# Group 0 of a fused transformer block in half-width units, its first weights in pieces, and a new order on one Trainium2 core

## The chip, the cores and the metric

The kernel runs on one core of one Trainium2 chip. The metric is the device time of one execution in microseconds (us); the number given for the kernel before is the median of three runs. Five engines work side by side, each through its own list of instructions in order: PE (matmuls; its weight loads are listed as PEld), DVE (vector), ACT (scalar activations and copies), POOL, and SP, which here only issues DMAs. Semaphores tie the engines together.

## The reference

x is [1, 2048, 512] in bf16. The vector c gives six modulation vectors of 512 (shift, scale and gate for each of two halves).

```
mod = (silu(c) @ w_mod)            # sa, ca, ga, sb, cb, gb
h = layernorm(x) * (1 + ca) + sa
x = x + ga * attention(h)          # 32 heads of 16, window of 8 positions at distance 2
h = layernorm(x) * (1 + cb) + sb
x = x + gb * ((gelu(h @ w_gate) * (h @ w_up)) @ w_down)     # F = 1792

# attention: q, k, v = h @ wqkv; position s looks at s, s-2, ..., s-14 (masked below 0)
logits = sum over d of q[s] * k[s - 2w] / 4;  attn = softmax over the 8 w
o = sum over w of attn * v[s - 2w];  result o @ wo
```

## The kernel before, in words

The 2048 positions go in four groups of 512 (number sg), each of four chunks of 128. The 512 channels of q, k and v are taken in four quarters j (every fourth channel, `j::4`), so that each quarter holds four channels of all 32 heads on 128 partitions. For each group:

- LN1: DVE and ACT take the statistics of a chunk (DVE BN_STATS2, L395, or ACT's sum and sum of squares, L378 and L384), POOL makes rstd, DVE writes xn (L435). PE transposes (or a DMA does), and DVE or ACT write hT with modulation (L487; for group 0, in two halves of 256 positions, L503 and L505).
- q, k, v: op `qp.sg.blk.j` (blk 0, 1, 2 for q, k, v) is four matmuls of 128x512 into one PSUM bank (L554); ACT evicts it (`qkv.sg.blk.j`; q L568, k L570, v L572). In group 0 quarters 0 and 1 of q are done by halves, 16 matmuls of 128x256 (L536, ops `qph`).
- logits: `pq.sg.j` on DVE multiplies q with eight shifted views of k (L617, 128x4096, 2.28 us each); `lp` on PE sums over channels and quarters with matmuls on a quarter of the array each (L631, 8 for each j, "quad" matmuls below). The last of a group's four is called `lp.sg`.
- softmax: DVE mask L643, max L648, subtract L654, ACT exp L659, DVE sum L664 (`s1.sg`), reciprocal L670 (`ri.sg`), product L675 (`p.sg`). SP writes the result to DRAM (`est`, L687) and reads it back spread out (`PT`, L694). v goes the same way (`vst` L591, `V4` L599).
- `pv.sg.j` on DVE (L706), `o.sg.j` on PE (L720, quad), oT on ACT (L731), `x1p.sg.c` on PE with wo (L741), x1 on DVE (L750), then LN2.
- FFN, 14 tiles n of 128 of F: `g.sg.n` and `u.sg.n` on PE (L771, four matmuls of 128x512 each), gelu on ACT (`gl`, L803) and a copy (`ub`, L810), their product on DVE (`hh.sg.n`, L821), and after all 14 the product with w_down (`y`, L783, L794), with the output on DVE (L828, L835) and its DMA.

The gates ga and gb are multiplied into wo and w_down: `woS` (L361), and `WdS0` to `WdS6` (L356), seven instructions of 128x1024, two for each of the tiles Wd0 to Wd2 and one for Wd3. Wd0, Wd1 and Wd2 have no buffers of their own: they take those of wqkv's three blocks (pool wA), so that each of their DMAs (L243) waits until PE has used that block for the last time.

Limits: four PSUM banks for matmul results (`mm`), two for transposes and others (`att`), one for logits; three buffers each for `gl` and `ub`; four for the products `pq` and `pv` (`prod`).

All of this is written as some 120 generators ("threads") of operations. `ORDER` (L18) is a list of thread numbers: the issuer takes the next operation of the thread that stands next in the list and emits it. So ORDER alone sets in what sequence each engine, and each DMA queue, gets its instructions; an operation's time and place otherwise follow from semaphores.

In the first microseconds the DMAs bring x for group 0 in two halves, the first two blocks of w_mod (0 the shift, 1 the scale), wqkv's q block, x of group 1, then k's and v's blocks. PE turns w_mod's blocks into modT and 1 + scale (matmuls of one column, L286; ACT writes scl L294 and modT L291).

## Time and profile before

| | us |
| --- | --- |
| three runs | 238.48, 236.38, 237.23 |
| median | 237.23 |
| span of the profiled execution, first to last instruction | 234.1 |
| its whole time | not on the page; the median is 3.1 above its span |
| PE / DVE / ACT busy in the span | 228.9 / 167.5 / 148.4 |
| first qkv matmul, last PE instruction's end (about) | 8.88, 231.3 |
| first gate matmul of the FFN (g.0.0) | 65.23 |
| granted TensorE clock | 0.999 |

How to read what follows: a row of the order of time gives start, length, engine, line, operation, output <- inputs, shape and type, and the count of merged instructions; in square brackets stands the idle time before it and what ended that. The pipelined matmuls overlap in the records, so the time of several is taken from start to start. In the table of stretches the columns are the stretch and its length, then busy time (and instructions) of PE, PEld, DVE, ACT and POOL, the granted clock, the DMA engines' share and GB/s.

### The profile page before, as it was taken

What the parts mean: (1) busy time and instruction counts of PE and PEld (TensorE: products, weight loads), DVE (VectorE), ACT (ScalarE), POOL (GpSimd) and SP (SyncE); (2) the same over time, 40 slices, a digit from 0 to 9 for tenths busy, and PEclk for the clock granted to TensorE, in tenths of its full rate; (3) what the DMA queues carried; (4) which work ended last, traced back from release to release, by engine and by line L of the source; (5) the groups of instructions that cost most, each with busy time, mean ns of one, the idle gap of its engine ahead of it and who ended that gap; (6) DMA issues with size and microseconds to landing.
All of it is one profiled execution on the core that took longest, in us unless ns stands there. A gap on an engine that the chain in (4) does not pass through costs nothing.

```text
span 234.1 us, 3657 instructions
## 1 busy us (share of the span) xinstructions
PE 228.9 (98%) x1382; PEld 107.2 (46%) x1382; DVE 167.5 (72%) x240; ACT 148.4 (63%) x282; POOL 24.7 (11%) x37
## 2 busy tenths in 40 slices
PE   7899999999999999999999999999999999999995
PEld 2755454444544444444444444444444444444443
DVE  4889999999998999989999989916642122123222
ACT  4999996968995749928556961563568721466400
POOL 3210230892100000100000010000100000000000
PEclk9999999999999999999999999999999999999999
DMA  6998869999368280054404634100071001000011
GB/s 214 385 332 295 244 224 221 301 329 408 159 188 235 97 276 3 1 115 134 114 0 128 243 91 97 40 0 22 0 71 45 0 22 42 6 0 1 21 48 45
DMA packets 30313, 30.42 MB, mean 130 GB/s; under 512 B 14936, under 2 KB 26200, under 8 KB 30296
## 3 DMA queue, kind: packets, MB, share of 16 engines
q1 hardware_dynamic: 29760, 29.67, 41.3%
q10 hardware_dynamic: 536, 0.53, 0.6%
q8 instruction: 11, 0.18, 0.3%
q14 instruction: 6, 0.05, 0.1%
HBM read 22.78 MB, written 5.31 MB: 120 GB/s over the span
## 4 chain that ended last, share of the span: by engine, by line
PE 84%; DVE 9%; DMA 3%; ACT 1%; SPq 1%; issue 0%
PE g_ps L771 21%; PE u_ps L771 21%; PE y_ps L783 19%; PE qkv_ps L554 9%; PE x_ps L741 6%; DVE pq L617 5%; PE o_ps L720 3%; DMA x<-in_A_x_dram 3%; PE LTp L631 2%; PE y_ps L794 1%; DVE xn L435 1%; DVE st L395 1%; ACT qT L568 1%; DVE mx L648 1%; DVE LTp L654 1%; DVE e L675 1%
## 5 line engine op out<-in xcount | busy, mean ns | idle before, releaser
L771 PE MATMUL g_ps<-h,Wg 128*128 128x512 bf16 x224 | 57.5, 379 | 0.0
L771 PE MATMUL u_ps<-h,Wu 128*128 128x512 bf16 x224 | 57.5, 379 | 0.0
L803 ACT ACTIVATE gl<-g_ps 128x512 bf16<-128x512 f32 x56 | 33.8, 605 | 24.3 <-PE g_ps L771 23.4
L783 PE MATMUL y_ps<-Wd,hht 128*128 128x512 bf16 x210 | 47.0, 379 | 0.0
L821 DVE TENSOR_TENSOR hht<-gl,ub 128x512 bf16<-128x512 bf16 x56 | 23.2, 420 | 31.8 <-ACT ub L810 31.6
L810 ACT CAST ub<-u_ps 128x512 bf16<-128x512 f32 x56 | 33.0, 592 | 17.1 <-PE u_ps L771 17.1
L554 PE MATMUL qkv_ps<-hT,wqkv 128*128 128x512 bf16 x184 | 42.0, 380 | 0.2 <-ACT gR L349 0.2
L617 DVE TENSOR_TENSOR pq<-qT,kT 128x4096 bf16<-128x4096 bf16 x16 | 36.3, 2284 | 0.3 <-ACT kT L570 0.3
L706 DVE TENSOR_TENSOR pv<-PT,V 128x4096 bf16<-128x4096 bf16 x16 | 36.0, 2285 | 0.2 <-PE LTp L631 0.2
L771 PEld LDWEIGHTS <-Wg 128*128 128x128 bf16 x224 | 21.7, 98 | 27.2 <-issue 1.7
L771 PEld LDWEIGHTS <-Wu 128*128 128x128 bf16 x224 | 21.8, 98 | 26.8 <-issue 0.8
L783 PEld LDWEIGHTS <-hht 128*128 128x128 bf16 x210 | 20.4, 98 | 25.2 <-issue 0.8
L554 PEld LDWEIGHTS <-wqkv 128*128 128x128 bf16 x184 | 20.2, 114 | 18.8 <-issue 2.4
L426 POOL TENSOR_TENSOR rstd<-rstd,neghalf 128x4 f32<-128x4 f32 (+1 forms) x9 | 8.7, 971 | 122.3 <-DVE rstd L415 68.7
L828 DVE TENSOR_TENSOR ot<-y_ps,x 128x512 bf16<-128x512 f32 x15 | 10.2, 686 | 15.9 <-PE y_ps L783 15.9
L750 DVE TENSOR_TENSOR x<-x_ps,x 128x512 bf16<-128x512 f32 x16 | 10.8, 684 | 7.1 <-PE x_ps L741 7.1
L741 PE MATMUL x_ps<-woP,oT 128*128 128x512 bf16 x64 | 15.3, 379 | 0.0
L395 DVE BATCH_NORM_STATS2 st<-x 128x6 f32<-128x512 bf16 x19 | 12.5, 678 | 2.5 <-DMA x<-in_A_x_dram 2.5
L487 ACT ACTIVATE h<-h,modT,scl 128x512 bf16<-128x512 bf16 x12 | 9.0, 808 | 8.1 <-DMA h<-xn 8.1
L587 POOL COPY vh<-vT 128x64 bf16<-128x64 bf16 x3 | 12.0, 3992 | 16.7 <-ACT vT L572 16.7
L731 ACT CAST oT<-o_ps 128x512 bf16<-128x512 f32 x16 | 9.2, 600 | 6.6 <-PE o_ps L720 6.6
L378 ACT ACTIVATE gl<-x 128x512 bf16<-128x512 bf16 x13 | 8.3, 650 | 6.8 <-DVE x L750 6.0
(77 smaller groups left out, 186.8 us busy)
## 6 DMA issues: line engine op xcount, KB each, us to landing
V<-vscr SPq DMA_DIRECT2D x16, 526.0 KB, 6.7
wm<-in_w_mod_dram SPq DMA_DIRECT2D x5, 512.0 KB, 8.5
vscr<-vT SPq DMA_DIRECT2D x4, 528.0 KB, 7.4
out_dram<-ot SPq DMA_DIRECT2D x15, 128.0 KB, 1.7
Wg<-in_B_w_gate_dram SPq DMA_DIRECT2D x4, 448.0 KB
Wu<-in_B_w_up_dram SPq DMA_DIRECT2D x4, 448.0 KB, 7.6
wqkv<-in_A_wqkv_dram SPq DMA_DIRECT2D x3, 512.0 KB, 7.1
x<-in_A_x_dram SPq DMA_DIRECT2D x3, 512.0 KB, 8.0
```

Of the source, the lines that this page charges most:

```text
L395: nc.vector.bn_stats(out=k["st", c4][:], in_=src()[:, c4, :])
L554: nc.tensor.matmul(ps[:], lhsT=wqkv[blk][:, dt, j::4], rhs=B["hT", sg][:, :, dt, :], start=(dt == 0), stop=(dt == DT - 1))
L587: yield Op("POOL", 0.2, lambda: nc.gpsimd.tensor_copy(out=vh[:], in_=B["vT", sg][:, :, SG:VR]), after=[f"qkv.{sg}.2.3"], fire=f"vh.{sg}")
L617: nc.vector.tensor_tensor(out=pq[:], in0=_ap(B["qT", sg][:, j, :], [[0, W], [1, SG]]), in1=_ap(kT[:, j, sg * SG + 2:sg * SG + 2 + SG], [[2 ...
L706: nc.vector.tensor_tensor(out=t[:], in0=_ap(B["PT", sg][:, 0, :], [[SG, 2], [0, 4], [1, SG]]), in1=_ap(v[:, j, 0, :], [[8, 2], [VR, 4], [1 ...
L741: nc.tensor.matmul(ps[:], lhsT=B["oT", sg][:, j, c4 * P:(c4 + 1) * P], rhs=woP[:, j, :], start=(j == 0), stop=(j == 3))
L750: nc.vector.tensor_tensor(out=x[:, c4, :], in0=B["x1ps", sg, c4][:], in1=x[:, c4, :], op=ALU.add)
L771: nc.tensor.matmul(ps[:], lhsT=Wt[:, dt, ft * P:(ft + 1) * P], rhs=B["h2T", sg][:, :, dt, :], start=(dt == 0), stop=(dt == DT - 1))
L783: nc.tensor.matmul(ps[:], lhsT=B["hh", sg, ft][:, c4 * P:(c4 + 1) * P], rhs=B["Wd", ft // 4][:, ft % 4, :], start=(ft == 0), stop=(ft == F ...
L803: nc.scalar.activation(out=gl[:], in_=B["g", sg, ft][:], func=ACT.Gelu_apprx_tanh)
L810: nc.scalar.copy(out=ub[:], in_=B["u", sg, ft][:])
L821: nc.vector.tensor_tensor(out=hh[:], in0=B["gl", sg, ft][:], in1=B["ub", sg, ft][:], op=ALU.mult)
```

## The change

- **Loads.** x of group 0 comes as chunk 0, chunk 1 and chunks 2 and 3. Blocks 0 and 1 of w_mod become one tile `wm01` in two pieces, 768 KB and 256 KB, on SP's queue (before: one block on ACT's queue and one on SP's). wqkv's q block comes in four pieces of 128 KB, with x of group 1 between the first and the other three.
- **Modulation.** One PSUM bank takes all eight columns of shift and scale; ACT writes the scale, DVE the shift. The exp table is loaded earlier.
- **Group 0's transposes** go chunk by chunk, both halves into `att` banks.
- **Group 0's q, k, v** go in 12 units (half h of 256 positions, block blk, pair of quarters u): 8 matmuls of 128x256 into one bank, which ACT evicts at once as 128x2x256 (`qu.h.blk.u`, `qe.h.blk.u`; four of the units are issued in single steps, `quf`). pq.0.0 is split into two halves; pq.0.1 needs the units u = 0 of both halves, pq.0.2 and pq.0.3 those with u = 1.
- **ORDER** is a new list for the whole program.

The diff, cut to its core:

```diff
-            yield Op("SP", 0.47, ldx(0, 0, 2), fire="x0.0", lat=1.0)
+            yield Op("SP", 0.47, ldx(0, 0, 1), fire="x0.0", lat=1.0)
+            yield Op("SP", 0.47, ldx(0, 1, 2), fire="x0.1", lat=1.0)
+            yield Op("SP", 0.47, ldwm01(0, 3), take=[SL["prod"]], fire="wmA", lat=1.9)
+            yield Op("SP", 0.47, ldwm01(3, 4), fire="wmB", lat=0.6)
...
+            for dt in DT0:
+                yield Op("SP", 0.47, ld(wqkv[0][:, dt, :], wq_v[:, dt, 0:D]), fire=f"wqkv0.{dt}", lat=0.35)
...
+        yield Op("PE", 0.82, cols(0, 3), after=["wmA", "scT"], take=[SL["mm"]], fire="mpA")
+        yield Op("PE", 0.28, cols(3, 4), after=["wmB"], give=[SL["prod"]], fire="mpB")
+        yield Op("ACT", 0.12, lambda: nc.scalar.add(out=scl[:, 0:4], in_=B["mp"][:, 4:8], add=1.0), after=["mpB"], fire="mod1")
+        yield Op("DVE", 0.12, lambda: nc.vector.tensor_copy(out=modT[:, 0:4], in_=B["mp"][:, 0:4]), after=["mpB"], give=[SL["mm"]], fire="mod0")
...
+    DT0 = (0, 2, 1, 3)
+    DT1 = (1, 2, 0, 3)
+    def unit_mm(h, blk, u, dt, start, stop):
+        if start:
+            B["qu", h, blk, u] = T("mm", [P, 2, 256], F32, "qkv_ps")
+        for jj in range(2):
+            nc.tensor.matmul(B["qu", h, blk, u][:, jj, :], lhsT=wqkv[blk][:, dt, 2 * u + jj::4],
+                             rhs=B["hT", 0][:, 2 * h:2 * h + 2, dt, :], start=start and jj == 0, stop=stop and jj == 1)
+    def unit(h, blk, u):
+        def f():
+            for n, dt in enumerate(DT0):
+                unit_mm(h, blk, u, dt, n == 0, n == 3)
...
+    def fine(h, blk, us, dts):
+        for n, dt in enumerate(dts):
...
+    def unit_ev(h, blk, u):
+        def g():
+            ps = B["qu", h, blk, u]
+            o, w = 2 * u, slice(h * 256, h * 256 + 256)
+            if blk == 0:
...
+                nc.scalar.copy(out=B["qT", 0][:, o:o + 2, w], in_=ps[:])
+            elif blk == 1:
+                nc.scalar.copy(out=kT[:, o:o + 2, 16 + h * 256:16 + h * 256 + 256], in_=ps[:])
+            else:
+                nc.scalar.copy(out=B["vT", 0][:, o:o + 2, VH + h * 256:VH + h * 256 + 256], in_=ps[:])
...
+        mm = [chain(fine(0, 0, (0, 1), DT0), unit(0, 1, 0), unit(0, 1, 1)), chain(*[unit(*a) for a in v0]),
+              chain(fine(1, 0, (0,), DT1), *[unit(*a) for a in q1[1:]], *[unit(*a) for a in v1])]
...
+    def qkd(sg, blk, j):
+        return [f"qe.{h}.{blk}.{j // 2}" for h in range(2)] if sg == 0 else [f"qkv.{sg}.{blk}.{j}"]
...
+            parts = ((0, 256), (256, 512)) if sg == 0 and j in SPLIT else ((0, SG),)
...
+                dep = [q for blk in range(2) for q in qkd(sg, blk, j)[:1 if c1 < SG else 2]]
-    1, 26, 2, 10, 0, 10, 2, 1, 2, 0, 2, 10, 10, 2, 10, 0, 10, 9, 10, 2, 9, 20, 9, 10, 20, 10, 18, 20, 10, 21,
...
+    29, 2, 1, 2, 3, 0, 17, 39, 29, 29, 29, 0, 0, 18, 39, 29, 29, 29, 29, 39, 29, 39, 39, 2, 2, 29, 29, 29, 29, 39,
```

What the new list moves is seen in the engines' own orders. First ACT in the evictions of group 0 (gl<-x are the sums and squares for later groups' LN1, hT the evictions of group 1's transposes). Before:

```order
L378 ACTIVATE gl,sums<-x 128x512 x2
L572 CAST vT<-qkv_ps 128x512 x3
L487 ACTIVATE hT<-hTp,modT,scl 128x4x128 x4
L572 CAST vT<-qkv_ps 128x512
L570 CAST kT<-qkv_ps 128x512
L349 CAST gR<-gR_ps 128x128
```

and changed:

```order
L586 CAST kT<-qkv_ps 128x2x256
L508 ACTIVATE hT<-hTp,modT,scl 128x4x128 x2
L588 CAST vT<-qkv_ps 128x2x256 x2
L508 ACTIVATE hT<-hTp,modT,scl 128x4x128 x2
L588 CAST vT<-qkv_ps 128x2x256 x2
L399 ACTIVATE gl,sums<-x 128x512
L586 CAST kT<-qkv_ps 128x2x256
L405 ACTIVATE gl,sums<-x,sums 128x512
```

In both, a k eviction comes last of group 0. Before it holds quarter 3 for all 512 positions; now it holds quarters 2 and 3 for the first half (unit qu.0.1.1, on PE too the last of group 0), behind one sum (L399) of a later chunk.

Then DVE around the softmax of group 1 (Wd<-Wd,gB are the scalings WdS, two for a tile; hht the FFN's products). Before:

```order
L664 TENSOR_REDUCE ssum<-LTp 128x128
L670 RECIPROCAL rinv<-ssum 128x128
L675 TENSOR_TENSOR e<-LTp,rinv 128x2x4x128
L617 TENSOR_TENSOR pq<-qT,kT 128x4096 x2
L821 TENSOR_TENSOR hht<-gl,ub 128x512 x3
L706 TENSOR_TENSOR pv<-PT,V_884 128x4096 x2
L821 TENSOR_TENSOR hht<-gl,ub 128x512 x2
L706 TENSOR_TENSOR pv<-PT,V_884 128x4096 x2
L356 TENSOR_TENSOR Wd_1099<-Wd_1099,gB 128x1024
```

and changed:

```order
L733 TENSOR_REDUCE ssum<-LTp 128x128
L377 TENSOR_TENSOR Wd_1129<-Wd_1129,gB 128x1024
L739 RECIPROCAL rinv<-ssum 128x128
L377 TENSOR_TENSOR Wd_1129<-Wd_1129,gB 128x1024
L744 TENSOR_TENSOR e<-LTp,rinv 128x2x4x128
L683 TENSOR_TENSOR pq<-qT,kT 128x4096 x2
L890 TENSOR_TENSOR hht<-gl,ub 128x512 x2
L377 TENSOR_TENSOR Wd_1131<-Wd_1131,gB 128x1024 x2
L890 TENSOR_TENSOR hht<-gl,ub 128x512
L775 TENSOR_TENSOR pv<-PT,V_1013 128x4096 x2
```

The first two scalings move from behind all four pv of group 1 to behind its ssum, ahead of ri.1, p.1 and the logits products of group 2, and the next two to ahead of pv.1.0.

Last SP's queue at the same place (escr<-e is est.1, PT its way back, gB the gate's load). Before:

```order
L687 DMA escr_117<-e 128x1024
L243 DMA Wd_1099<-in_B_w_down_dram 128x4x512
L298 DMA gscr_115<-gR 4x128
L694 DMA PT<-escr_117 128x4x128 x2
L303 DMA gB<-gscr_115 128x512
L243 DMA Wd_1140<-in_B_w_down_dram 128x4x512
```

and changed:

```order
L316 DMA gB<-gscr_115 128x512
L318 DMA modc<-gscr_114 128x4x1
L253 DMA Wd_1129<-in_B_w_down_dram 128x4x512
L253 DMA Wd_1131<-in_B_w_down_dram 128x4x512
L756 DMA escr_117<-e 128x1024
L763 DMA PT<-escr_117 128x4x128 x2
L662 DMA V_1013<-vscr_109 128x1x2104 x2
```

The gate gB and the first two Wd tiles now come ahead of est.1, and half of group 1's V behind it. On PE the last q matmuls of group 3, which free wqkv's first block, stay in the second place before the first FFN matmul, as before.

## The prediction

> **What bounds the kernel now.** I read the page's head and its chain first, then the stretches in one table, and then the order of time on each engine at the two places where the new order changes what stands behind what.

> ```profile
> PE 228.9 (98%) x1382; PEld 107.2 (46%) x1382; DVE 167.5 (72%) x240; ACT 148.4 (63%) x282; POOL 24.7 (11%) x37
> ...
> PE 84%; DVE 9%; DMA 3%; ACT 1%; SPq 1%; issue 0%
> ...
> 8.88:36.00 27.12, 26.71 (x227) 14.77 (x225) 26.17 (x44) 26.32 (x61) 5.37 (x7) 1.00 0.87 285
> 36.00:65.39 29.39, 29.39 (x205) 14.63 (x202) 29.09 (x31) 23.91 (x47) 12.81 (x5) 1.00 0.82 275
> 65.39:97.03 31.64, 31.64 (x194) 13.69 (x192) 29.96 (x33) 24.11 (x51) 0.00 (x0) 1.00 0.48 148
> 149.98:234.10 84.12, 81.24 (x412) 37.12 (x412) 27.05 (x58) 36.85 (x64) 1.01 (x1) 1.00 0.11 23
> ```

> The columns behind the length are PE, PEld, DVE, ACT and POOL. TensorE is busy in all of every stretch from the first qkv matmul at 8.88 on shown here but for 0.41 us and the tail, at full clock. So whatever PE waits from there on is added to the end, and nothing gives it back but less PE work. The share of 72% for VectorE hides that up to 97 us it is as full as PE (29.09 of 29.39, 29.96 of 31.64): until then the two run side by side with no slack, and an instruction that makes DVE wait delays everything behind it in DVE's order, PE's inputs among it. After 150 us DVE is idle two thirds of the time, too late to help. The span is 234.10; the page does not give this execution's whole time, and I put 237.23 - 234.10 = 3.13 us around the span, the median of the runs.

> **The start.** wqkv1, which group 0's k needs, has the same 3.15 MB in the queues up to its end in both kernels: x0, w_mod's two blocks, wqkv0, x1 and itself; pieces change their order, not the sum. The first matmul on it waited for just that:

> ```profile
> 7.70 0.61 PE L472 MATMUL hTp<-ident,xn 128*128 128x128 bf16 x8
> 8.88 1.91 PE L536 MATMUL qkv_ps<-hT,wqkv 128*128 128x256 bf16 x16
> 10.63 2.10 PE L554 MATMUL qkv_ps<-hT,wqkv 128*128 128x512 bf16 x9
> 11.39 1.08 PEld L554 LDWEIGHTS <-wqkv 128*128 128x128 bf16 x6 [0.22 <-DMA wqkv<-in_A_wqkv_dram]
> ```

> Both kernels do the same work ahead of it (24 half-quarters of q). An earlier first matmul therefore buys at most the 0.22 of this wait and a little of the landing (-0.3). Against it, half 1's evictions now stand on DVE and ACT behind statistics of x1, which must land first: up to +0.5. I take +0.2, nearer the loss, since those evictions have no other cover.

> The work itself: (10.63 - 8.88) / 16 = 0.109 us for 256 columns; 96 of these are 10.5 us, against 16 of them and 40 of 512 columns at twice that, 10.4: +0.1. Halving the columns costs as good as nothing. Evictions stay at 12 with 512 elements each.

> **Quad stretches.** Matmuls on a quarter of the array come in stretches, and entering or leaving one costs:

> ```profile
> 19.72 0.59 PE L554 MATMUL qkv_ps<-hT,wqkv 128*128 128x512 bf16 x2
> 20.25 0.41 PE L344 MATMUL gR_ps<-wm,scB 128*32 128x128 bf16 x16
> 20.48 1.04 PE L631 MATMUL LTp<-pq,Mph 128*32 128x512 bf16 x16
> 21.45 0.84 PE L554 MATMUL qkv_ps<-hT,wqkv 128*128 128x512 bf16 x3
> ```

> Two matmuls of 0.216 took 0.53 before the stretch (+0.10), and sixteen quads, four side by side, took 0.97 instead of 4 x 0.216 = 0.86 (+0.11): some 0.22 for a stretch. The order has 12 stretches instead of 15, four fewer ahead of g.0.0 and one more behind it: -0.9 and +0.2.

> **Hole 1: pq.0.2 waits for the last unit.** Before, the logits products took the quarters as they came:

> ```profile
> 13.50 2.29 DVE L617 TENSOR_TENSOR pq<-qT,kT 128x4096 bf16<-128x4096 bf16 x1 [0.32 <-ACT kT L570]
> 17.59 4.49 DVE L617 TENSOR_TENSOR pq<-qT,kT 128x4096 bf16<-128x4096 bf16 x2
> 22.60 2.27 DVE L617 TENSOR_TENSOR pq<-qT,kT 128x4096 bf16<-128x4096 bf16 x1
> 14.28 0.59 ACT L568 CAST qT<-qkv_ps 128x512 bf16<-128x512 f32 x1 [0.28 <-PE qkv_ps L554]
> 15.14 0.59 ACT L570 CAST kT<-qkv_ps 128x512 bf16<-128x512 f32 x1 [0.28 <-PE qkv_ps L554]
> 18.28 2.82 ACT L487 ACTIVATE hT<-hTp,modT,scl 128x512 bf16<-128x512 bf16 x4
> 20.95 0.63 ACT L572 CAST vT<-qkv_ps 128x512 bf16<-128x512 f32 x1
> 21.41 0.65 ACT L570 CAST kT<-qkv_ps 128x512 bf16<-128x512 f32 x1
> 22.67 0.70 ACT L378 ACTIVATE gl<-x 128x512 bf16<-128x512 bf16 x1
> 23.29 0.79 ACT L384 ACTIVATE gl<-x,sums 128x512 bf16<-128x512 bf16 x1
> 24.16 0.61 PE L631 MATMUL LTp<-pq,Mph 128*32 128x512 bf16 x8
> 24.93 0.40 PE L631 MATMUL LTp<-pq,Mph 128*32 128x512 bf16 x4 [0.15 <-DVE pq L617]
> ```

> The k quarter that is evicted last, at 21.41, was needed by pq.0.3 alone, at 22.60. A unit carries two quarters: now the last one evicted (half 0, k, quarters 2 and 3) is needed by pq.0.2 and pq.0.3. On PE it comes ninth from the first wqkv1 matmul at 11.7: 9 x 0.875 and two sets of 8 transposes at 0.44 end at 20.5. On ACT it stands behind the same evictions as before and one sum and one square of x more (0.62 by the pitch from 22.67 to 23.29, and as much again to 0.79), which fill some 0.7 of the idle time that ACT had there (0.28 twice in these rows): start about 21.9, and, an eviction's 0.5 later, k ready at 22.4. DVE has by then finished pq.0.1, at 17.59 + 4.49 / 2 = 19.84 less the 0.32 wait = 19.5 (its other work up to here is the same to a few tenths). So DVE idles 2.9 us; bounds 1.4 (ACT takes the unit as soon as PE is done) and 3.3. pq.0.2 ends at 24.6, pq.0.3 at 26.85, against 24.87. PE, with two units of group 1, two lp and one gate block behind the last unit, stands at lp.0.2 at 23.4: it waits 1.2, then after 0.45 another 1.8 at lp.0.3: 3.0, in place of the 24.93 - 24.16 - 0.45 = 0.3 here before. **+2.6** (1.1 to 3.0).

> **Hole 2: the scaling of Wd stands ahead of the softmax.** WdS0 multiplies the first half of the first w_down tile; that tile takes wqkv0's buffer, so its DMA can be issued only when the last q matmul of group 3 is done.

> ```profile
> 61.31 1.23 DVE L664 TENSOR_REDUCE ssum<-LTp 128x128 f32<-128x1024 f32 x1
> 62.57 0.95 DVE L670 RECIPROCAL rinv<-ssum 128x128 f32<-128x128 f32 x1
> 63.56 1.22 DVE L675 TENSOR_TENSOR e<-LTp,rinv 128x1024 bf16<-128x1024 f32 x1
> 64.70 4.48 DVE L617 TENSOR_TENSOR pq<-qT,kT 128x4096 bf16<-128x4096 bf16 x2
> 69.11 0.42 DVE L821 TENSOR_TENSOR hht<-gl,ub 128x512 bf16<-128x512 bf16 x1
> 64.81 0.33 SPq L687 DMA_DIRECT2D escr<-e  x1
> 65.24 0.39 SPq L243 DMA_DIRECT2D Wd<-in_B_w_down_dram  x1
> L356 DVE TENSOR_TENSOR Wd<-Wd,gB x7: 679/684/685, 81.1 to 96.9; 128x1024 bf16<-128x1024 bf16 x7
> DMA to landing us min/median/max: 3.6/6.1/7.0
> 63.50 1.89 PE L554 MATMUL qkv_ps<-hT,wqkv 128*128 128x512 bf16 x8
> 65.23 1.03 PE L771 MATMUL g_ps<-h,Wg 128*128 128x512 bf16 x4
> 66.09 0.38 PE L771 MATMUL u_ps<-h,Wu 128*128 128x512 bf16 x1
> 68.01 0.60 ACT L803 ACTIVATE gl<-g_ps 128x512 bf16<-128x512 f32 x1
> ```

> Before, the Wd DMA went at 65.24, landed 3.6 us later, and DVE first touched Wd at 81.1: 12 us of cover. Now WdS0 follows s1.1, which ends at 62.54 + 2.0 (hole 1) = 64.5. The new g.0.0 is at 65.23 + 0.2 + 0.1 - 0.9 + 2.6 = 67.2, the last q matmul one unit (66.09 - 65.23 = 0.86) earlier, 66.35; with 3.6 less some 0.4 for the 0.26 MB of escr that stood just ahead before, Wd lands at about 69.6 (69.2 to 70.3). DVE idles 5.1 us (4.7 to 5.8) with ri.1, p.1, pq.2.0, pq.2.1, the first hh and group 1's pv queued behind.

> No row here shows an instruction of DVE overtaking one that waits, and the sum goes by DVE's own order; could DVE pass the wait, rival (a) below would come of it. [...] For the landing, the bare 3.6 us of the row would make hole 2 0.4 longer (244.7). [...]

> hh.0.0 then ends at 69.6 + two WdS (1.36) + 0.99 + 1.14 + 4.41 + 0.4 = 77.9. Until then three gl buffers and four PSUM banks let PE run five g/u pairs, 67.2 + 5 x 1.73 = 75.8; g.0.5 needs a bank that ACT frees after hh.0.0, at 78.5: PE waits 2.7. Behind come WdS2, WdS3 and only then pv.1.0: by the same sums PE waits 1.25 more at o.1.1 and 0.95 at o.1.3. **+4.9.** Bounds: 3 if the later two waits are covered, 6 if Wd lands at 70.3.

> **The sum:** 0.2 + 0.1 - 0.9 + 2.6 + 4.9 + 0.2 = +7.1: span 241.2, time **244.3 us**.

> **The rivals.**
> (a) Hole 2 does not reach PE. For: PE has five pairs queued, and Wd could land earlier. Against: it must land by 64.5, so be issued by 60.9, and the last q matmul is at 66.35. All but the 4.9 stays: 237.23 + 2.2 = 239.4.
> (b) Not slower: PE's own list decides. The start gains its 0.3, the stretches 0.7 net, and both waits of DVE end while PE has other work: 237.2 - 0.3 + 0.1 - 0.7 = 236.3. For: PE has been dense in every stretch so far. It decides only if k of the last unit is ready by 20.6 (1.8 earlier than I work out) and Wd by 66; the rows put ACT's list and the DMA's 3.6 us against both.
> (c) The stalls breed: DVE, 7 us late with 30 us of 31.6 filled, makes PE wait 1 to 1.5 at each of the three later groups' pv too: 244.3 + 3.5 = 247.8. Against: PE is late by the same 7 us.

> **How the numbers follow.** Forecast 0.55, (a) 0.20, (b) 0.15, (c) 0.10. A measurement of this kernel tells about 1% from no change, 234.9 to 239.6. (b) gives a third to faster (0.05) and two thirds to same; (a) lies at the edge and is halved: same 0.10 + 0.10 = 0.20, slower 0.75. Bounds of the terms give 241 to 246.5 for the forecast alone; down to (a) and most of the way to (c) the range is 238.5 to 247.5.

> **What would show it.** In the changed profile: DVE's pq waiting 2 to 3 us for ACT's kT near 20 us, and PE's LTp for DVE's pq; DVE's Wd scaling waiting 4 to 6 us for a DMA near 65 to 70 us, and PE's g_ps waiting near 76; PE as dense as before elsewhere. If DVE's idle time is there but PE's is not, it is (a). If kT comes before 20.6 or Wd before 66, the order's places are harmless and I am wrong from there on.

## The result, and the profile after

The changed kernel takes 244.95 us (median of four runs, 243.60 to 246.24) against 237.57 for the kernel before: ratio 1.032, interval 1.025 to 1.039. The forecast of 244.3 us, a ratio of 1.028, lies within it. Its working does not hold, though: one of its two large terms was not there, and others that it had at next to nothing, or not at all, filled the gap.

Here the runs list the span beside the time, with 1.7 to 1.75 us around it in each. The profiled execution of before (span 234.1) was therefore some 1.4 us faster than the median that the forecast was made against, and the two profiled spans, 243.9 and 234.1, differ by 9.8, while the medians differ by 7.4.

The head of the page and the table of stretches, in the same rows as for the kernel before:

```profile
PE 232.9 (95%) x1422; PEld 113.0 (46%) x1422; DVE 168.9 (69%) x242; ACT 150.6 (62%) x281; POOL 15.3 (6%) x37
```

```profile
8.88:36.00 27.12, 24.20 (x222) 17.76 (x220) 20.80 (x37) 21.05 (x50) 3.01 (x5) 0.87 0.76 257
36.00:65.39 29.39, 26.71 (x207) 12.99 (x206) 25.55 (x22) 20.97 (x42) 4.15 (x5) 1.00 0.86 256
65.39:97.03 31.64, 31.64 (x187) 14.88 (x186) 31.42 (x39) 24.80 (x47) 1.62 (x4) 1.00 0.53 152
149.98:243.90 93.92, 91.28 (x459) 41.56 (x457) 33.91 (x67) 41.60 (x70) 1.01 (x1) 1.00 0.12 30
```

PE is idle for 2.9 us of the first stretch (before: 0.4) and for 2.7 of the second (before: none), and the granted clock of the first is 0.87 instead of 1.00. From 65 us on it is as dense as before. The first gate matmul stands at 75.14 against 65.23: the whole difference of the two executions, 9.9 us, is there by then.

PE's rows at the start, and the clock of four short stretches:

```profile
6.25 0.17 PE L333 MATMUL scp<-ident,c 4*128 4x4 bf16 x1
7.90 0.99 PE L305 MATMUL modT_ps<-scT,wm 128*128 128x1 bf16 x32 [1.48 <-DMA wm<-in_w_mod_dram]
10.32 1.06 PE L555 MATMUL qkv_ps<-hT,wqkv 128*128 128x256 bf16 x4
```

```profile
8.80:10.00 1.20, 1.20 (x15) 0.76 (x13) 0.75 (x3) 0.77 (x3) 0.00 (x0) 0.73 1.10 375
10.00:12.00 2.00, 2.00 (x14) 1.48 (x13) 1.51 (x4) 1.97 (x7) 0.00 (x0) 0.50 1.07 378
28.00:30.00 2.00, 0.38 (x12) 0.07 (x8) 2.00 (x2) 1.12 (x3) 0.00 (x0) 0.96 0.80 254
30.00:34.00 4.00, 4.00 (x32) 1.74 (x32) 3.67 (x9) 0.66 (x2) 1.01 (x1) 0.59 0.41 136
```

The modulation waits until 7.90 for w_mod, and all 32 one-column matmuls come after it (before: 16 of them, at 7.28). The first qkv matmul is at 10.32 instead of 8.88, and PE, which waited 1.48 us for w_mod, then runs at half its clock (the third column from the right). The same happens again after the idle time near 29 us. In finer stretches the clock is 0.50 from 9.36 to 12.77 and from 29.84 to 33.25 us.

Hole 1, on DVE, ACT and PE:

```profile
25.38 4.53 DVE L683 TENSOR_TENSOR pq<-qT,kT 128x4096 bf16<-128x4096 bf16 x2 [3.26 <-ACT kT L586]
24.06 0.72 ACT L399 ACTIVATE gl<-x 128x512 bf16<-128x512 bf16 x1
24.68 0.66 ACT L586 CAST kT<-qkv_ps 128x512 bf16<-128x512 f32 x1
27.72 0.61 PE L700 MATMUL LTp<-pq,Mph 128*32 128x512 bf16 x8 [1.30 <-DVE pq L683]
29.96 0.62 PE L700 MATMUL LTp<-pq,Mph 128*32 128x512 bf16 x4 [1.62 <-DVE pq L683]
```

DVE waits 3.26 us for the last k eviction and PE 1.30 and 1.62 at lp.0.2 and lp.0.3: place and size are those of the forecast (2.9; 1.2 and 1.8).

Hole 2, on DVE, SP and PE:

```profile
71.67 1.23 DVE L733 TENSOR_REDUCE ssum<-LTp 128x128 f32<-128x1024 f32 x1
72.81 0.68 DVE L377 TENSOR_TENSOR Wd<-Wd,gB 128x1024 bf16<-128x1024 bf16 x1
69.26 5.58 SPq L253 DMA_DIRECT2D Wd<-in_B_w_down_dram  x2
66.48 5.34 PE L616 MATMUL qkv_ps<-hT,wqkv 128*128 128x512 bf16 x24
75.14 1.03 PE L840 MATMUL g_ps<-h,Wg 128*128 128x512 bf16 x4
```

No bracket stands behind WdS0 at 72.81: it did not wait. Its DMA went at 69.26. The 24 matmuls from 66.48 begin with v's quarters 1 to 3, 12 of them, which end at 66.48 + 12 x 0.216 = 69.07, 0.19 before the first Wd DMA; the last q matmul is one unit before 75.14 and ends at 74.3. The row of the two DMAs ends at 74.84, and one takes some 0.4, so the second went 0.2 after that q matmul. So the first Wd tile took the buffer of wqkv's v block, which is done first, and the second that of the q block.

And a wait that the forecast did not have, on SP, ACT and PE:

```profile
46.68 5.35 SPq L476 DMA_TRANSPOSE hT<-xn  x1
46.16 2.29 ACT L636 CAST vT<-qkv_ps 128x512 bf16<-128x512 f32 x4 [1.71 <-DMA vscr<-vT]
55.54 1.52 ACT L508 ACTIVATE hT<-hT,modT,scl 128x512 bf16<-128x512 bf16 x2 [3.04 <-DMA hT<-xn]
46.80 4.48 PE L616 MATMUL qkv_ps<-hT,wqkv 128*128 128x512 bf16 x20 [0.50 <-ACT vT L636]
56.40 0.38 PE L616 MATMUL qkv_ps<-hT,wqkv 128*128 128x512 bf16 x1 [0.98 <-ACT hT L508]
57.97 0.38 PE L616 MATMUL qkv_ps<-hT,wqkv 128*128 128x512 bf16 x1 [0.49 <-ACT hT L508]
```

```profile
36.72 3.06 SPq L455 DMA_TRANSPOSE hT<-xn  x1
```

The second fence is the kernel before. Group 3's transpose now starts at 46.68, 10 us later, and PE waits for its result (four waits, 2.1 us in all, two of them shown) and 0.5 for v.

### The profile page after: what moved, and what is told of

Same layout as the page of the kernel before. It is cut to its first block, busy times and chain, and to the rows that moved or that the text cites. A ratio compares the mean times of both kernels' runs of the same rounds, so it can differ in the third digit from the quotient of the medians.

```text
span 243.9 us, 3743 instructions
## 1 busy us (share of the span) xinstructions
PE 232.9 (95%) x1422; PEld 113.0 (46%) x1422; DVE 168.9 (69%) x242; ACT 150.6 (62%) x281; POOL 15.3 (6%) x37
## 4 chain that ended last, share of the span: by engine, by line
PE 78%; DMA 8%; ACT 6%; DVE 4%; issue 1%; SPq 1%; POOL 0%; ACTq 0%
PE g_ps L840 20%; PE u_ps L840 20%; PE y_ps L852 19%; PE x_ps L810 6%; PE qkv_ps L616 4%; DMA hT<-xn 4%; PE o_ps L789 3%; DMA wm<-in_w_mod_dram 2%; PE LTp L700 2%; ACT hT L508 2%; DVE pq L683 2%; DMA vscr<-vT 2%; PE qkv_ps L555 2%; PE y_ps L863 1%; ACT kT L586 1%
## 5 line engine op out<-in xcount | busy, mean ns | idle before, releaser
L683 DVE TENSOR_TENSOR pq<-qT,kT 128x4096 bf16<-128x4096 bf16 (+1 forms) x17 | 36.3, 2161 | 3.8 <-ACT kT L586 3.8
L616 PE MATMUL qkv_ps<-hT,wqkv 128*128 128x512 bf16 x144 | 34.0, 387 | 2.6 <-ACT hT L508 2.1
L616 PEld LDWEIGHTS <-wqkv 128*128 128x128 bf16 x144 | 16.2, 115 | 18.4 <-issue 5.3
L555 PE MATMUL qkv_ps<-hT,wqkv 128*128 128x256 bf16 x96 | 12.0, 284 | 0.0
L700 PE MATMUL LTp<-pq,Mph 128*32 128x512 bf16 x128 | 8.9, 395 | 2.9 <-DVE pq L683 2.9
```

What stands on the lines that cost most here:

```text
L555: nc.tensor.matmul(B["qu", h, blk, u][:, jj, :], lhsT=wqkv[blk][:, dt, 2 * u + jj::4], rhs=B["hT", 0][:, 2 * h:2 * h + 2, dt, :], start=st ...
L616: nc.tensor.matmul(ps[:], lhsT=wqkv[blk][:, dt, j::4], rhs=B["hT", sg][:, :, dt, :], start=(dt == 0), stop=(dt == DT - 1))
L683: nc.vector.tensor_tensor(out=B["pq", sg, j][:, :, c0:c1], in0=_ap(B["qT", sg][:, j, c0:c1], [[0, W], [1, c1 - c0]]), in1=_ap(kT[:, j, sg ...
L700: nc.tensor.matmul(B["LT", sg][H * g:H * g + H, 4 * t:4 * t + 4, :], lhsT=M[:], rhs=B["pq", sg, j][:, 4 * t:4 * t + 4, g * P:(g + 1) * P], ...
```

## The experiments

The theory from these rows: what is lost lies ahead of the first gate matmul, in three places: the idle and therefore slow PE at the start, hole 1 with the slow clock behind it, and SP's queue. The rival is the forecast's: hole 1 and the place of WdS0. The ratio given for each is to the kernel before, run beside it; the changed kernel's own is 1.032. In the diffs a line is a stretch of one engine's sequence. Some of its names: scp (PE) and scT (ACT) bring silu(c) into place for the modulation's matmuls mp; LN1.3.x0 to .x3 are the four xn of group 3 and LN1.3.t is its DMA transpose; vst writes v to DRAM, V4 and pt read V and PT back; ga, gst and mc move the gates and the later modulation vectors; wo, x and wm are loads.

**WdS0 to WdS3 back behind pv.1** (undoes hole 2's cause alone).

```diff
 DVE: s1.1
-DVE: WdS0, ri.1, WdS1, p.1, pq.2.0, pq.2.1, hh.0.0, hh.0.1, WdS2, WdS3
+DVE: ri.1, p.1, pq.2.0, pq.2.1, hh.0.0, hh.0.1
...
 DVE: pv.1.2, pv.1.3
+DVE: WdS0, WdS1, WdS2, WdS3
```

> The changed kernel (median 244.95) with WdS0 to WdS3 moved back behind all four pv of group 1 on DVE; nothing else moves. The forecast's theory: their early place costs 4.9 us, so about 240. The rival, read from the changed profile, where WdS0 starts at 72.81 without any wait: the place costs nothing, so 244 to 246, and DVE's Wd rows still show no wait.

1.034 (1.025 to 1.042): nothing gained. A gain of 4.9 us would have given 1.011, far outside, so the forecast's theory falls; the interval alone would leave room for a microsecond or two, but in the changed profile no scaling waits.

**The last unit early** (undoes hole 1 alone).

```diff
-PE: qu.1.0.1, qu.1.1.1, LN1.1.t0, qu.0.2.0, ..., qu.1.2.1, qu.0.1.1
+PE: qu.1.0.1, qu.0.1.1, qu.1.1.1, LN1.1.t0, qu.0.2.0, ..., qu.1.2.1
-ACT: qe.1.0.1, qe.1.1.1, ..., qe.1.2.1, LN1.3.sa1, qe.0.1.1
+ACT: qe.1.0.1, qe.0.1.1, qe.1.1.1, ..., qe.1.2.1, LN1.3.sa1
```

> The changed kernel with the unit qu.0.1.1 and its eviction moved ahead, right behind qu.1.0.1 and qe.1.0.1, so that pq.0.2 need not wait for the last eviction of group 0. Theory: hole 1 costs the 2.6 us net that PE waits at lp.0.2 and lp.0.3, and 1.4 more because PE runs at a lower granted clock from 30 to 34 us after that wait; both go: 241, DVE's pq waits under 0.7 us in all and the clock of that stretch is 1.00. Rival one: the wait goes but the lower clock has another cause: 242.4. Rival two: the time is only handed on to the later wait for group 3's hT (2.8 us in the changed profile grows): 244 to 245.

1.015 (1.009 to 1.020), so 4.1 us of the 7.4, give or take 2 by the two intervals. The second half of pq.0.0 and the three other products are now one block behind a wait of 0.58:

```profile
18.10 7.83 DVE L681 TENSOR_TENSOR pq<-qT,kT 128x2048 bf16<-128x2048 bf16 x4 [0.58 <-ACT kT L584]
```

The 4.1 is above the 2.6 that PE waited net, though not beyond the noise. The clock from 28 to 34 us was 1.00 in this profile: the slow clock behind the wait went with it, as the first theory had it. Half clock for the 3.41 us from 29.84 to 33.25 can cost up to 1.7 us; by that estimate the 2.6 become up to 4.3.

**Six more warm-up matmuls** between scp and w_mod's first matmul.

```diff
-    pl.spawn(warmup(10, 15))
+    pl.spawn(warmup(10, 21))
-PE: scp, mpA
+PE: scp, warm x6, mpA
```

> The changed kernel with six more warm-up matmuls of 128x512 on PE between scp and the first w_mod matmul, where PE idles 1.5 us before 7.90. Theory: the granted clock of 0.5 to 0.8 from 8.8 to 14 us comes of that idle time and costs the first 7 qkv matmuls 0.105 us each, and the warm-ups and transposes ahead of them some 0.4: with PE kept busy the clock is 1.00 there and the time falls by about 1.1, to 243.8. Rival: the first k matmul is bound by the evictions of hT and not by PE's clock, and hole 1 behind it by ACT's list: the clock is 1.00 but the time stays at 245.

1.021 (1.015 to 1.027), 2.7 us, give or take 2, where 1.1 was expected. Its clock:

```profile
10.00:12.00 2.00, 2.00 (x24) 1.96 (x23) 2.00 (x7) 1.97 (x7) 0.00 (x0) 1.00 1.09 385
30.00:34.00 4.00, 4.00 (x26) 2.25 (x25) 4.00 (x8) 3.63 (x8) 0.64 (x1) 1.00 0.07 22
```

The clock is full at the start, which was the theory, and also from 30 to 34, although PE waits at lp.0.2 and lp.0.3 as long as before (1.29 and 1.62 us). So the idle time there does not always bring the slow clock, and in this profile the experiment removed more than its own place.

**w_mod in two tiles on two queues**, as in the kernel before.

```diff
+            yield Op("ACT", 0.46, ldwm(1, nc.scalar), take=[SL["h2"]], fire="wm1", lat=3.2, dma=True)
...
-            yield Op("SP", 0.47, ldwm01(0, 3), take=[SL["prod"]], fire="wmA", lat=1.9)
-            yield Op("SP", 0.47, ldwm01(3, 4), fire="wmB", lat=0.6)
+            yield Op("SP", 0.5, ldwm(0), take=[SL["h2"]], fire="wm0", lat=1.4)
```

> The changed kernel with w_mod's first two blocks as two tiles again, block 1 on ACT's queue and block 0 on SP's as in the kernel before, and its columns taken block by block; x0, wqkv0 in pieces, the units and the rest of the order as changed. Theory: the one tile in two pieces on SP's queue makes the modulation 1.2 us later (9.14 against 7.89), and so the first qkv matmul (10.32 against 8.88); with two queues that comes back: the first qkv near 9.1, PE's idle time ahead of it is shorter, the time 1.2 to 2 lower, 243 to 243.8. Rival: the small pieces ahead of it keep the DMA engines from being full, so w_mod is as late on two queues: 245.

1.045 (1.039 to 1.052): slower by 3 us more. Both theories missed it. PE's row names what held it:

```profile
8.66 0.97 PE L303 MATMUL modT_ps<-scT,wm 128*128 128x1 bf16 x32 [2.39 <-ACT scT L335]
```

scT stands on ACT behind the sums of x0's last chunk, and those came later (6.66 instead of 5.21 us), as they waited longer for that chunk; that the other queue's w_mod block went ahead of it is the likely reason, not a tried one.

**The same with scp and scT early**, so that block 1 need not wait.

```diff
-PE: warm x12, scp, mpA, mpB, th0.0, th0.1, warm x3
+PE: warm x6, scp, warm x8, mpA, mpB, th0.0, th0.1, warm
-ACT: LN1.0.sa3, LN1.0.sq3, ..., scT
+ACT: scT, LN1.0.sa3, LN1.0.sq3
```

> The two w_mod tiles on two queues again, and besides scp behind six warm-up matmuls instead of twelve and scT on ACT ahead of the sums of x0 instead of behind them, as in the kernel before, so that block 1's columns are done before block 0 lands and PE is warm. All else as changed (x0 and wqkv0 in pieces, units, order). With two tiles alone the modulation came later, as PE waited 2.4 us for scT behind those sums. Theory: the start's loss is made by the order around scT and the idle PE, not by the pieces: first qkv at 9.0 to 9.4, clock 1.00 from there on, 241 to 242.5. Rival: the pieces keep the DMA engines from being full and w_mod lands as late: first qkv not under 10, 244 or more.

1.038 (1.032 to 1.043), the first qkv at 10.60: the theory on the start's order fell, as its rival said. Now the chain went through x0 itself, on DVE and ACT:

```profile
6.41 0.69 DVE L414 BATCH_NORM_STATS2 st<-x 128x6 f32<-128x512 bf16 x1 [1.82 <-DMA x<-in_A_x_dram]
9.98 1.02 ACT L524 ACTIVATE hT<-hTp,modT,scl 128x256 bf16<-128x256 bf16 x2 [1.43 <-DVE modT L350]
```

The shift's copy to modT stands on DVE behind all four xn, and these wait for x0's last piece. The two parts of the start are made for each other: pieces of x0 ahead of one w_mod tile, and the shift on DVE.

**Group 3's xn and its transpose early** (undoes the wait for hT alone).

```diff
-DVE: p.0, pq.1.0, pq.1.1, LN1.3.x0, .x1, .x2, .x3
+DVE: p.0, LN1.3.x0, .x1, .x2, .x3, pq.1.0, pq.1.1
-SP: vst.1, pt.0.0, pt.0.1, V4.0.2, V4.0.3, LN1.3.t
+SP: vst.1, LN1.3.t, pt.0.0, pt.0.1, V4.0.2, V4.0.3
```

> The changed kernel with the xn of group 3 (four instructions on DVE) ahead of pq.1.0 and pq.1.1 instead of behind them, and the DMA transpose of group 3 on SP ahead of PT's two reads. Theory: in the changed profile PE waits 2.8 us between 55 and 59 us for ACT's hT of group 3, whose DMA transpose starts at 46.68 and lands 8.8 us later, because xn comes 9 us later than before on DVE; issued 4 to 5 us earlier, that wait goes, less up to 1 us that PT is later: 242 to 243.5. Rival: PE then waits the same time for pv and x1p of group 0, since DVE is as late as before: 244 to 245.5.

1.032 (1.026 to 1.037): nothing, as the rival said, and the rows show why. On SP and DVE:

```profile
42.16 4.51 SPq L474 DMA_TRANSPOSE hT<-xn  x1
46.77 1.07 SPq L761 DMA_DIRECT2D PT<-escr  x2
49.87 8.90 DVE L773 TENSOR_TENSOR pv<-PT,V 128x4096 bf16<-128x4096 bf16 x4 [3.10 <-DMA PT<-escr]
```

The transpose occupies SP's queue for 4.5 us, PT goes 2.4 us later than in the changed kernel, and DVE waits for it.

**Warm-ups and early unit together** (the edits of both).

> The six more warm-up matmuls and the early unit qu.0.1.1 together. Apart they brought 2.8 and 4.3. Theory A: they are separate costs and add up: 237.5 to 238.5. Theory B: part of both is the same slow clock after PE's wait near 30 us, which each removes: 1.4 is counted twice, 239 to 240.

1.008 (1.005 to 1.010). Apart they brought 1.73 and 1.13 points of the ratio (a point is 2.4 us), together 2.43 of the 2.86. The 1.0 us between lies between the two theories and within the noise, so it decides for neither. The clock says more: 3.41 us at half clock take 0.007 off the mean granted clock of an execution of 244 us. The four executions of the changed kernel have means of 0.979 to 0.993, so by this estimate one to three such stretches each (the profiled one, at 0.986, shows two); the ten of this kernel have 1.00 (0.999 once), so none.

**All three places, with two w_mod tiles** (the edits of the early unit, the early xn and transpose, and the early scT).

> All three places undone by order: qu.0.1.1 early, group 3's xn and its transpose early, and the start with two w_mod tiles, scp and scT early. The halves, the units, the pieces of x0 and wqkv0 and the rest of the new order, with WdS0 in its early place, stay. Theory: these three are the whole loss, and three fewer quad stretches are worth 0.7: 235.5 to 237.5, the kernel before within 1%. Rival: the units or the rest of the new order cost something that no row names yet: 239 or more. A third, the forecast's hole 2: with DVE no longer late WdS0 now has to wait for its DMA, some 3 to 5 us near 63: 239 to 241 with that wait in the rows of Wd.

1.017 (1.012 to 1.022): the start's and the transpose's edits, which did not help alone, did not help here. Rival one's figure, but not its reason: the first qkv was at 11.39 in its profile. WdS0 did not wait here either (ssum ended as WdS0 began).

**SP's queue, first try**, on top of warm-ups and early unit.

```diff
-SP: V4.0.1, wo2, est.0, mc3, wo3, vst.1, pt.0.0, pt.0.1, V4.0.2, V4.0.3, LN1.3.t
+SP: vst.1, V4.0.1, V4.0.2, V4.0.3, est.0, mc3, wo1, wo2, wo3, pt.0.0, pt.0.1, LN1.3.t
-DVE: pq.1.0, pq.1.1, LN1.3.x0, .x1, .x2, .x3
+DVE: pq.1.0, LN1.3.x0, .x1, .x2, .x3, pq.1.1
```

> The six warm-ups and the early unit (238.66 in the last comparison, where the kernel before was 237.12), and besides on SP: vst.1 and the three V loads of group 0 ahead of est.0, the wo pieces behind it, group 3's DMA transpose right behind PT; on DVE group 3's xn ahead of pq.1.1. Theory: what is left of the loss is PE's 2.5 us wait for group 3's hT and 0.9 for v, because SP's queue is one line in which a transpose of 4 to 5 us and late wo pieces stand ahead of what others wait for (xn early alone gained nothing since the transpose then held PT back by 2.4 us): 235 to 236.5, not slower than the kernel before. Rival: the transpose lands as late wherever it stands, because the DMA engines are shared: 238 to 239.

1.017 (1.015 to 1.020), worse than without it. The waits for hT and v were gone from ACT's rows, but DVE had two new ones, and PE, which waited 2.71 us behind them, then ran at half its pace again from 47 us on (the clock is 0.89 from 45 to 60 us; the 16 quads from 48.05 took 1.71 us from start to start, 0.86 with the warm-ups and the early unit alone):

```profile
42.67 1.23 DVE L381 TENSOR_TENSOR woP<-woP,gB 128x2048 bf16<-128x2048 bf16 x1 [2.87 <-DMA woP<-in_A_wo_dram]
44.95 8.90 DVE L774 TENSOR_TENSOR pv<-PT,V 128x4096 bf16<-128x4096 bf16 x4 [1.05 <-DMA PT<-escr]
```

**The last v matmul of group 3 late**, behind the last q matmul, so that no block of wqkv comes free before q's.

```diff
+    QKV3 = [(0, 0), (1, 0), (2, 0), (2, 1), (2, 2), (0, 1), (1, 1), (0, 2), (1, 2), (0, 3), (2, 3), (1, 3)]
...
-        for n, (blk, j) in enumerate(QKV):
+        for n, (blk, j) in enumerate(QKV3 if sg == 3 else QKV):
```

> The changed kernel with the last v matmul of group 3 moved from the middle to the last but one place of group 3's matmuls (its eviction with it). The changed trace shows the first Wd DMA issued at 69.26, 0.1 us after that v matmul ends, and not after the last q matmul at 74: the tile takes the buffer of wqkv's v block. Theory: with it moved, the Wd DMA goes at about 74, WdS0 waits 4 to 5 us for it, and the forecast's hole 2 is really there: up to 4.9 more, 248 to 250. Rival one: the wait is there but PE's queue of gate and up tiles covers it: 245 to 247. Rival two: the DMA goes as before and nothing changes: 245.

1.051 (1.049 to 1.054), 4.6 us more than the changed kernel. On DVE, SP and PE:

```profile
74.64 0.69 DVE L377 TENSOR_TENSOR Wd<-Wd,gB 128x1024 bf16<-128x1024 bf16 x1 [4.29 <-PE u_ps L841]
71.07 1.24 SPq L253 DMA_DIRECT2D Wd<-in_B_w_down_dram  x2
70.02 2.75 PE L617 MATMUL qkv_ps<-hT,wqkv 128*128 128x512 bf16 x12
83.34 1.02 PE L841 MATMUL g_ps<-h,Wg 128*128 128x512 bf16 x4 [1.82 <-ACT gl L873]
88.94 0.61 PE L790 MATMUL o_ps<-pv,Mph 128*32 128x512 bf16 x8 [1.00 <-DVE pv L776]
94.34 0.62 PE L790 MATMUL o_ps<-pv,Mph 128*32 128x512 bf16 x8 [0.69 <-ACT oT L801]
```

This is hole 2 as forecast: WdS0 waits 4.3 us (the table names PE; the DMA issued at 71.07 lands 3.4 us later), and PE waits at g.0.5, o.1.1 and o.1.3, the three places that the working gave (3.5 us together; it had 4.9). The last q unit is the first of the three from 70.02 and ends at 70.02 + 4 x 0.216 = 70.88, 0.19 before the DMA: now that v's block is done later, the first Wd tile takes q's, as the forecast had it for the changed kernel. Its chain from there on was right, and its price near (4.6, give or take 2); what it had wrong is which block comes free first. DVE kept its order behind the wait: ri.1 began at 75.25, behind WdS0 at 74.64. The expectation, which had the tile wait for v's block, was wrong there too.

**The kernel before with an idle PE**: without eight of its warm-up matmuls.

```diff
-PE: warm x6, scp, warm x8, mp1, mp0
+PE: warm x6, scp, mp1, mp0
```

> The kernel before, without the eight warm-up matmuls between scp and the first w_mod matmul, so that PE idles about 2 us from 4.0. Theory: the lower granted clock in the changed kernel's start comes of PE's idle time alone; here too the clock falls under 0.9 between 8 and 14 us, and the time rises by 1 to 3: 238.2 to 240. Rival: the clock belongs to the changed kernel's other work; here it stays at 1.00 and the time at 237.

1.013 (1.009 to 1.016), 3 us. A stretch, and PE's first qkv:

```profile
4.00:8.00 4.00, 0.78 (x20) 0.61 (x21) 3.39 (x13) 3.25 (x8) 1.52 (x2) 1.00 1.08 376
10.00:12.00 2.00, 2.00 (x15) 1.56 (x13) 1.53 (x5) 1.34 (x5) 0.00 (x0) 1.00 1.09 386
```

```profile
10.44 3.10 PE L534 MATMUL qkv_ps<-hT,wqkv 128*128 128x256 bf16 x16
```

The 16 matmuls take 13.37 - 10.44 = 2.93 us, 0.18 each against 0.109, so too few matmuls ahead of them are enough for a slow PE. But it is not quite the changed kernel's case. The first six warm-ups take some 0.44 us each in both profiles of the old kernel, half the pace of the 0.216 later on; then the old kernel's eight transposes at 7.70 take 0.055 each, while here those at 8.35 still take 0.10. So PE had not yet come to its full pace here, while the changed kernel's had (its transposes at 8.76 take 0.055) and fell back. The clock column stays at 1.00 throughout, so the expected sign in it did not come; the pitch of the matmuls shows the slow PE.

**SP's queue as in the kernel before**, with group 3's xn early on DVE, on top of warm-ups and early unit.

```diff
-SP: wm2, x3
+SP: wm2, wo1, wo2, wo3, x3
-SP: V4.0.0, ga, gst3, wo1, V4.0.1, wo2, est.0, mc3, wo3, vst.1, pt.0.0, pt.0.1, V4.0.2, V4.0.3, LN1.3.t
+SP: V4.0.0, V4.0.1, ga, gst3, vst.1, est.0, V4.0.2, mc3, pt.0.0, pt.0.1, LN1.3.t, V4.0.3
-DVE: pq.1.0, pq.1.1, LN1.3.x0, .x1, .x2, .x3
+DVE: pq.1.0, LN1.3.x0, .x1, .x2, .x3, pq.1.1
```

> The six warm-ups, the early unit, group 3's xn ahead of pq.1.1, and SP's queue around est.0 in the sequence of the kernel before: the wo pieces ahead of x3, two V loads of group 0 early, vst.1 ahead of est.0, one V load ahead of PT, the transpose behind PT, the last V load behind it. In the last try the wait for hT was gone, but woS waited 2.9 us for the wo pieces and pv 1.1 us for PT, which stood behind them and behind three V loads. Theory: these were the price of my placing and with them gone nothing of the loss before the first gate matmul is left but the 1 us later start: 235.5 to 237.5 beside 236 to 237 for the kernel before, within 1% of it. Rival: DVE or PE finds another wait of 2 us or more in the same stretch: 238.5 or more.

0.997 (0.994 to 1.000): no longer slower than the kernel before. In the second stretch PE is dense again, and the evictions of v and hT wait for no DMA:

```profile
36.00:65.39 29.39, 29.24 (x218) 14.61 (x217) 29.25 (x31) 24.27 (x48) 17.05 (x7) 1.00 0.82 254
```

```profile
43.99 0.58 ACT L635 CAST vT<-qkv_ps 128x512 bf16<-128x512 f32 x1 [0.28 <-PE qkv_ps L615]
48.49 1.55 ACT L507 ACTIVATE hT<-hT,modT,scl 128x512 bf16<-128x512 bf16 x2
```

The profiled execution is the longest of the twelve (238.75 us; the others took 235.73 to 237.78). In it w_mod's matmuls start only at 9.18, PE waits 2.34 us for them in spite of the six warm-ups, and the clock is 0.94 from 8.88 to 36 us, as much as some 3.3 us at 0.50 would take off by an estimate from these numbers. So the warm-ups did not keep the clock up in this execution, where w_mod came later than they last.

Step by step, as differences of the ratios: the early unit 1.73 points, the warm-ups 0.70 on top of it, SP's queue with the early xn 1.05 on top of both; 3.48 points of the 3.19 that the change lost. Each step is known to 0.4 to 0.9 points, and the order counts: with the warm-ups first they are worth 1.13 and the early unit 1.30 (3.1 us). The surplus, 0.3 points or 0.7 us with an interval that touches zero, has the sign and size of the forecast's fewer quad stretches (-0.6 with the narrower matmuls), but it does not measure them: the loads still come in pieces here, and the first qkv matmul is later than before (9.73 with the warm-ups and the early unit, 11.42 here, 8.88 before).

## Why the prediction was right, and where it was wrong

- **What bounds.** Right: PE and DVE have no slack up to 97 us, and what PE waits there stays. After the first gate matmul the two executions run alike.
- **Hole 1.** Right in place and mechanism: 2.9 us of PE's wait against 3.0. The wait's own price is not disproved either: 2.6 forecast, 2.6 net in the rows, 3.1 (give or take 1.5) measured on top of the warm-ups. What the working lacked is the slow clock behind the wait, up to 1.7 more; undone alone, the place was worth 4.1.
- **Hole 2.** Wrong. The step that failed is "that tile takes wqkv0's buffer, so its DMA can be issued only when the last q matmul of group 3 is done". The trace of before had the Wd DMA at 65.24, just behind the last matmul of group 3; but it also stood in SP's queue just behind escr at 64.81, which suffices to explain it. Two things ended at the same time, and the working took the one that made the larger term. In the changed kernel v's block is done 5 us before q's, and the first Wd tile takes that. The early scaling waited for nothing; made to wait for q's block by the late v matmul, it cost 4.6 against 4.9. The 0.4 us that the working took off the landing's 3.6 is shown by no run; the shortest landing of a Wd DMA was 3.3 us in the changed kernel and 3.4 with the late v matmul.
- **The start.** Wrong: +0.2 forecast. The first qkv came 1.4 later, and PE was at half its clock up to 12.77; with more warm-ups, 2.7 us returned, 1.7 with hole 1 undone. That "pieces change their order, not the sum" was about bytes, not about when they land: to 8.88 us the DMA engines moved 234 GB/s after and 272 before (the last column):

```profile
0.00:8.88 8.88, 6.15 (x48) 2.71 (x49) 4.51 (x14) 4.97 (x11) 3.29 (x21) 1.00 0.78 234
```

```profile
0.00:8.88 8.88, 7.01 (x64) 3.62 (x65) 4.79 (x16) 5.59 (x13) 3.39 (x22) 1.00 0.81 272
```

  That is 0.34 MB less. The size of it varies: the other profiles with the changed loads have 232 to 252 GB/s there, those with w_mod on two queues 256 to 258, the old kernel without warm-ups 274. Whether the pieces or the single queue made it is open: two queues brought back a small part at most, and x0 and wqkv0 in whole pieces were not tried.
- **SP's queue.** Missing. The forecast followed pq and WdS on DVE and did not ask what is late next: xn of group 3, moved behind pq.1.1, and three of the wo pieces, moved from the first 13 us to both sides of est.0; the transpose of xn and these loads all pass through SP. 2.5 us with the other two places mended.
- **Quad stretches and widths.** The count was right (15 stretches before and 12 after in the profiles, 8 and 4 of them ahead of g.0.0). The price of -0.6 is neither disproved nor shown: the -0.7 at the end holds whatever else the last kernel gains or loses.

So +7.1 was 0.2 + 2.6 + 4.9 - 0.6 on paper, and 4.1 + 1.7 + 2.5 - 0.7 = 7.6 on the chip (7.4 by the medians). The second sum is one of successive differences, so it must come out at the loss; the agreement with the first is luck, since a term of 4.9 that was not there stood in for the slow clock, the later start and SP's queue. Rival (a), hole 1 alone with hole 2 absorbed, was right that hole 2 does not reach PE, and missed the time by 5.5 us for want of the other two.

## What to carry to other kernels

When a DMA starts just as two things end, its start does not say which of them it waited for; find another instruction that separates them (here, which block's last reader had long been done) before a term is built on it. A new order has to be read on the DMA-issuing queue as carefully as on the compute engines: a slow issue there is a wait for everybody behind it (here 4.5 us of a transpose, and PT 2.4 us later). A tensor engine that is left idle for a microsecond or two may pay twice, in the wait and in the slow clock behind it (here 1.5 us of waiting, then 3.41 us at a clock of 0.50); six more matmuls on anything kept the clock at 1.00 here, as long as they lasted as long as the wait.
